# Stores of half one's sums spread over two units, x's sums and splits in another order, attention in bank 7 at a unit's first beat

## The chip, the cores and the metric

The kernel runs on one core of one Trainium2 chip. The metric is the device time of one execution in microseconds (us). Lower is better. Four compute engines work side by side, each on its own stream of instructions in program order: PE (TensorE, the matmuls), DVE (VectorE), ACT (ScalarE) and POOL (GpSimd). SP (SyncE) issues all of this kernel's DMA transfers, also in program order. Engines wait for each other by semaphores.

## The reference

A layer mixes an attention branch with a feed-forward branch, gate by gate. S = 2048 rows, D = 576, 32 heads of 18, four segments of 512 rows, 4608 hidden columns. Everything is float32.

```python
g = sigmoid((x * gate_w).sum(-1, keepdims=True))
# A: causal attention inside a segment, plus a memory of the segments before
for s in range(4):
    p = softmax(q_s @ k_s.T * scale + mask)
    a_dot = p @ v_s
    a_mem = (phi(q_s) @ M) / (phi(q_s) @ z + 1e-6)
    o = sigmoid(beta) * a_mem + (1 - sigmoid(beta)) * a_dot
    M, z = M + phi(k_s).T @ v_s, z + phi(k_s).sum()
a = concat(o) @ wo
# B: feed forward
b = (silu(x @ w_gate) * (x @ w_up)) @ w_down
out = g * a + (1 - g) * b
```

## The kernel before, in words

All float32 products are made of three cheaper ones: an operand is split into a high part (a copy on ACT that rounds) and a low part (a subtraction on DVE: `tensor_sub(lo, src, hi)`). A split is therefore always one ACT and one DVE instruction. The function `split` records both as L132 and L133, whatever is split.

The program has three stages. The first one (to about 221 us) makes q, k, v, the memory, and the splits of half of x. The second, which is the long one, runs the feed-forward branch with attention threaded through it. The third multiplies attention by `wo` and mixes.

**The second stage.** It has two halves: half one works on x's segments 2 and 3, half two on segments 0 and 1. Each half has 36 units, f = 0 to 35, one for each 128 hidden columns. A unit makes gate and up products of 1024 rows by a scheme of seven products (Strassen's): `seven(t, j)` is six matmuls of 512 columns (L1015) and one for the rest of the rows (L1018), on the operand `ops[j]` of the weights (tiles `wo_`, one DMA of 256 KB each where they are fetched from scratch memory `wc`, L709) and on `XO[j]` of x (tiles `xo`). The seven operands of x are sums of four pieces of x, split into high and low. A unit consists of eight beats: after each step the function `tick()` issues what is due. The ticks of a unit are numbered k = 0 to 7. `defer(n, fn)` puts a step n beats ahead.

**Down products.** Every third unit, at q = f % 3 = 0, sixteen groups for the three units before are put in a list (`feed`). A group is nine matmuls of 320 or 256 columns (L862) into one PSUM bank; DVE then adds the bank to the sum `ya` in SBUF (L872), which frees the bank. Two or three groups are run in a beat by the list SHARE.

**Attention.** A generator gives one step per beat or so: scores into a bank (`s_bank`, L724), a maximum over the bank on DVE (L730), exponentials on ACT (L742), a mask on POOL (L750), a split into halves on DVE and POOL (L756, L757), a transposing DMA (L761), and after five banks the products with v (`v_unit`, L772, L773).

**Banks.** PSUM has eight. `seven` uses 0, 1 and 2. Down groups take from (3, 4, 7) the one that was taken longest ago. Attention takes from (5, 6), when there are no groups from all five of (5, 6, 7, 3, 4), and, while all sixteen groups are still listed, from (5, 6, 7) (`ts_tile`). PE waits where a bank's last content is not read yet.

**Between the halves.** After unit 35 of half one, sixteen groups are left. They run in ten extra beats (BREAK). In the last unit and these beats the operands of x for half two are made by `x_second`: `load` (L986) fetches the eight pieces, `total` (L991) makes a sum on POOL, `parts` splits a piece or a sum, and the tables LOADS, SUMS and PARTS of (beat, z, piece or operand) say at which beat each is issued. Beat 0 of these tables is the first beat of unit 35, beat 8 the first extra one, beat 18 the first of half two. z says which half of the 256 rows of the contraction. The pieces with z = 1 lie in tiles `wo_`, whose places the weights of half two take next. In the first beat of half two, `tick` stores all eight tiles of half one's sums (`ffd<-ya`, L1056), and then fetches the seventh operand of that unit.

Of the kernel before, what the change touches and what calls it, by code (L numbers as in the profile page):

```python
# [27 lines left out]
FT = 36  # L28
# [7 lines left out]
CH = 3  # L36
# [12 lines left out]
SHARE = (0, 0, 2, 2, 3, 3, 3, 3)  # L49
BREAK = 10  # L50
LOADS = ((-3, 0, 0), (-2, 0, 1), (3, 1, 0), (4, 1, 3), (4, 0, 3), (5, 0, 2), (5, 1, 1), (6, 1, 2))
SUMS = ((2, 0, 1), (9, 0, 4), (10, 1, 1), (11, 1, 4), (13, 1, 2), (14, 1, 6), (17, 0, 2), (18, 0, 6))
PARTS = ((1, 0, 0), (4, 0, 1), (10, 1, 0), (12, 1, 5), (12, 1, 3), (13, 1, 1), (14, 1, 2), (15, 1, 4), (16, 1, 6),
         (16, 0, 5), (17, 0, 3), (18, 0, 2), (19, 0, 4), (20, 0, 6))
FIRST = (9, 10, 11, 15, 16, 17, 18)
SLOT = (0, 3, 2, 1, 4, 6, 5)
RPOS = (0, 1, 4, 2, 5, 6, 3)
# [9 lines left out]
def gated_mix(ctx, tc, xT, xrest, wf, wfr, wfh, wd, wv, wo, beta, cmask, ident, bmask, out):  # L67
    nc = tc.nc
# [43 lines left out]
    y_tile = banks(2)  # L112
    taken = {}
    clock = [0]

    def soonest(ids, held):
        n = min(ids, key=lambda i: taken.get(i, 0))
        clock[0] += 1
        taken[n] = clock[0] + held
        return n  # L120

    def ts_tile(shape=(P, L)):
        ids = (5, 6, 7, 3, 4) if not groups else (5, 6, 7) if groups[0][0] < FT // CH - 1 and len(groups) == 16 else (5, 6)
        return ps.tile(list(shape), F32, name=f"bank{soonest(ids, HELD)}")

    def group_tile(shape=(P, L)):
# [2 lines left out]
    groups = []  # L129
# [85 lines left out]
    def w_load(f, u):  # L215
        r = raw_tile().rearrange("p (k n) -> p k n", n=P)
        nc.sync.dma_start(r, wf[f][:, u, 0:4])
        return r
# [30 lines left out]
    def r_fetch(f):  # L249
        nc.sync.dma_start(f32(rhs[f % 2][:96]).rearrange("p j n -> p (j n)"), rc[f // 4, :, f % 4])  # L250
# [437 lines left out]
    with ExitStack() as st:  # L688
# [238 lines left out]
        def c_tr(o, me):  # L927
            if me is not None:
                nc.gpsimd.tensor_add(o[:, 0:D], o[:, 0:D], me)
            nc.gpsimd.tensor_copy(o[:, 576:640], o[:, 512:576])  # L930
            ta = half_tile([P, 4, P])
            for k in range(4):
                nc.tensor.transpose(ta[:, k], o[:, P * k:P * k + P], idt)
            tb = lone_tile([P, P])
            nc.tensor.transpose(tb, o[:, 512:640], idt)
            oh = cps[0].tile([P, 4, P], F32R, name="oh")
            ol = cps[0].tile([P, 4, P], F32R, name="ol")
            os_ = cps[0].tile([P, P], F32R, name="os")
            split(oh, ol, ta)
            xs_split(os_, tb)  # L940
            r = []
            for k in range(4):
                r += [oh[:, k], ol[:, k], oh[:, k]]
            return r + [os_, os_]


        stores = []
# [28 lines left out]
        def feed(half, f):  # L976
            return [(f // CH, i, hf, hs, ds, yas[half], half) for i in range(8) for hf in range(2)]

        def x_second(new, rest):
# [3 lines left out]
            def load(z, q):  # L983
                b, kt = ((0, z), (1, z), (0, 2 + z), (1, 2 + z))[q]
                r[z, q] = wop.tile([P, L], F32, name="wo_") if z else raw_tile()[:, :L]
                nc.sync.dma_start(r[z, q], xT[HALF[1][b], :, kt])  # L986

            def total(z, j):
                c, d, e, g = (r.get((z, q)) for q in range(4))
                o, p, q = {1: (c, d, c), 4: (d, g, d), 2: (g, g, c), 6: (e, e, g)}[j]  # L990
                nc.gpsimd.tensor_sub(o, p, q)  # L991

            def parts(z, j):
                new[j][z] = x_slot(SLOT[j], z)
                split(new[j][z][:, 0], new[j][z][:, 1], r[z, (0, 0, 3, 2, 1, 3, 2)[j]])

            def fetch(j):
                rest[j] = xr_tile(j)
                nc.sync.dma_start(f32(rest[j]), xrd[j])

            todo += [(o, lambda z=z, q=q: load(z, q)) for o, z, q in LOADS]
            todo += [(o, lambda z=z, j=j: parts(z, j)) for o, z, j in PARTS]
            todo += [(o, lambda z=z, j=j: total(z, j)) for o, z, j in SUMS]
            todo += [(6 + j, lambda j=j: fetch(j)) for j in range(7)]
# [19 lines left out]
        for pos, (half, f) in enumerate(seq):  # L1024
            if f == 0:
                yas[half] = yp.tile([P, 8, D], F32, name="ya")
            q = f % CH
            nxt = seq[pos + 1] if pos + 1 < len(seq) else None
            if q == 0 and f:
                groups += feed(half, f - 1)  # L1030
            plan = []
            if not nxt:
                plan.append((3, lambda: early.append(c_tr(*tiles.pop(0)))))
            if nxt:
                plan += w_fetch(nxt[1]) if nxt[0] and nxt[1] < KEPT else w_make(*nxt)
                if nxt != (0, 1):
                    plan.append((1 if nxt[1] else 10, lambda f=nxt[1]: r_fetch(f)))
                for n, h in enumerate(BLOCKS.get(pos, ())):
                    plan += r_block(h, 4 * n)
                if f + 2 < FT:  # L1040
                    wraw_of[f + 2] = [None, None]
                    for u in range(2):
                        plan.append(((2, 5)[u] if f or not half else 5 + u, lambda u=u, f=f: wraw_of[f + 2].__setitem__(u, w_load(f + 2, u))))
            if pos == FT - 2:
                X2, XR2 = [[None, None] for _ in range(7)], [None] * 7
                plan += [(o + 8, fn) for o, fn in x_second(X2, XR2)]
            for o, fn in plan:
                defer(o + 1, fn)
            step = [0]

            def tick():
                k = step[0]
                step[0] += 1
                if k == 0:
                    while stores:
                        nc.sync.dma_start(*stores.pop(0))  # L1056
                if half == 0:
                    if (q, k) in ((0, 3), (1, 3), (2, 2)):
                        draw[f] = d_load(f)
                    if (q, k) in ((1, 1), (1, 7), (2, 4)):  # L1060
                        g = f - 1 if k == 1 else f
                        ds[half, g] = d_split(g, draw.pop(g))
                elif (q, k) in ((1, 0), (1, 2), (2, 1)):
                    g = f - 1 if k == 0 else f
                    ds[half, g] = d_fetch(g)
                beat(k, half)

            ops, rem = wops.pop((half, f)), rhs[f % 2]
            hh = fp.tile([P, 2, L], F32R, name="hh")
            hl = fp.tile([P, 2, L], F32R, name="hl")  # L1070
            hs[half, f] = hh, hl
            a, y, xx = a_tile(), y_tile(), x_tile()
            p5, sg0, sg1 = (row_tile() for _ in range(3))
            seven(a, 0)
            nc.scalar.activation(xx, a, AF.Copy)  # L1075
            tick()
            seven(y, 1)
            nc.scalar.activation(p5, y, AF.Copy)
            tick()
            seven(a, 2, False)  # L1080
            y = y_tile()
            nc.vector.tensor_add(y, a, p5)
            tick()
            seven(xx, 3, False)
            nc.scalar.activation(sg0, xx, AF.Copy)  # L1085
            tick()
            seven(a, 4, False)
            xx = x_tile()
            nc.scalar.activation(xx, a, AF.Copy)  # L1089
            nc.vector.tensor_add(p5, a, p5)  # L1090
            tick()
            nc.scalar.activation(sg0, sg0, AF.Silu)  # L1092
            seven(y, 5, False)
            nc.scalar.activation(sg1, y, AF.Silu)
            if f < FT - 1:
                exp_table()
            tick()
            tick()
            seven(xx, 6, False)
            nc.vector.tensor_mul(sg0, xx, sg0)  # L1100
            nc.vector.tensor_mul(sg1, p5, sg1)
            if q == CH - 1:
                defer(2, lambda t=(hh[:, 0], hl[:, 0], sg0): split(*t))
            else:
                split_by(2, hh[:, 0], hl[:, 0], sg0)
            split_by(3, hh[:, 1], hl[:, 1], sg1)
            tick()
            assert not groups
            if f == FT - 1:
                groups += feed(half, f)  # L1110
                if half == 0:
                    for n in range(BREAK):
                        beat(None if n > 1 else n)
                        if n == 0:
                            down_parts([groups.pop(0) for _ in range(3)], CH - 1, CH)
                    XO, XR = X2, XR2
                    assert not groups
# [98 lines left out]
```

## Time and profile before

| | |
|---|---|
| median of 3 runs | 1736.47 us (1733.69 to 1738.83) |
| the profiled execution: its own time | 1734.02 us |
| its span from first to last instruction | 1732.2 us |
| granted TensorE clock, mean | 0.999 |
| busy: PE, DVE, ACT, POOL | 1713.1, 1373.7, 1092.4, 936.7 us |
| half one's last unit, the extra beats, half two's first unit | 912 to 925, 925 to 947.7, 947.7 to 965.9 us |

A row of the timeline gives start, duration, engine, line, operation, written and read tiles, and in brackets the idle time of the engine before it with what ended it. A matmul's end is modelled: the next one on PE starts 0.23 us after a matmul of 512 columns, though that one's row says 0.39. Rows that follow each other on one line and tile are merged (x6).

### The profile page before, as it was taken

To read this page: it belongs to the slowest core of one execution; us is meant where nothing else is said; L and a number is where in the kernel's file an instruction comes from. 1 tells how busy PE (TensorE), PEld (TensorE's weight loads), DVE (VectorE), ACT (ScalarE), POOL (GpSimd) and SP (SyncE) were. 2 spreads that over 40 slices of the span, in tenths; PEclk is the share of its full clock that TensorE was granted. 3 is DMA by queue.
4 is the path that set the end of the run, shared out by engine and by line. 5 is a ranking of instruction groups with operands and counts; after the bars stand their busy time and mean duration, and the time that the engine had idled before them with its cause. 6 is when DMAs were issued, how large, how long until landed. Compare 5 with 4: busy or idle time off the path is not lost.

```text
span 1732.2 us, 34907 instructions
## 1 busy us (share of the span) xinstructions
PE 1713.1 (99%) x11868; PEld 1479.3 (85%) x11868; DVE 1373.7 (79%) x3231; ACT 1092.4 (63%) x2195; POOL 936.7 (54%) x1194
## 2 busy tenths in 40 slices
PE   9999999999999999999999999999999999999999
PEld 7899978888888888887888788888888888888899
DVE  6667588888898889898989677788788777888655
ACT  7766585776677577667756756665765576566511
POOL 4424645666666556565666455555555555555221
PEclk9999999999999999999999999999999999999999
DMA  8654499999898898897979976876778677766544
GB/s 285 227 194 154 146 311 191 223 218 193 208 227 194 178 213 198 190 194 200 206 150 260 273 161 146 183 180 157 157 181 181 137 161 182 163 144 166 160 146 137
DMA packets 524002, 328.05 MB, mean 189 GB/s; under 512 B 411184, under 2 KB 460336, under 8 KB 523824
## 3 DMA queue, kind: packets, MB, share of 16 engines
q1 hardware_dynamic: 523824, 325.83, 76.6%
q8 instruction: 93, 1.52, 0.4%
q14 instruction: 85, 0.70, 0.1%
HBM read 165.76 MB, written 76.09 MB: 140 GB/s over the span
## 4 chain that ended last, share of the span: by engine, by line
PE 80%; ACT 6%; DVE 6%; DMA 3%; issue 2%; POOL 1%; SPq 1%; DVEq 0%; ACTq 0%; POOLq 0%
PE bank L1015 31%; PE bank L862 25%; PE bank L155 10%; PE bank L1018 5%; PE bank L724 4%; PE bank L772 2%; PE bank L773 1%; ACT L1092 1%; PE bank L410 1%; DVE scr L730 1%; DVE hl L957 1%; DVE p L756 1%; PE bank L456 1%; ACT L1008 1%; DVE xo L133 1%
## 5 line engine op out<-in xcount | busy, mean ns | idle before, releaser
L757 POOL TENSOR_TENSOR p<-pe,p 128x512 f16<-128x512 f32 x320 | 374.0, 1169 | 451.0 <-DVE p L756 431.3
L862 PE MATMUL bank<-dw,hh 128*128 128x320 f32 (+1 forms) x2304 | 489.7, 305 | 2.6 <-DVE ya L872 2.1
L862 PEld LDWEIGHTS bank<-dw,hh 128*128 128x128 f32 x2304 | 380.5, 190 | 16.7 <-DVE ya L872 5.7
L742 ACT ACTIVATE pe<-bank,mb 128x512 f32<-128x512 f32 (+3 forms) x512 | 246.0, 522 | 218.7 <-DVE mb L730 213.3
L862 PE MATMUL bank<-dw,hl 128*128 128x320 f32 (+1 forms) x1152 | 340.3, 295 | 0.2 <-DVE hl L133 0.2
L730 DVE CUSTOM_DVE_ANT_0 scr<-bank,cm 128x512 bf16<-128x512 f32 (+3 forms) x512 | 246.5, 481 | 7.8 <-PE bank L724 1.1
L862 PEld LDWEIGHTS bank<-dw,hl 128*128 128x128 f32 x1152 | 217.9, 189 | 0.4 <-DVE hl L133 0.4
L872 DVE TENSOR_TENSOR ya<-bank,ya 128x320 f32<-128x320 f32 x352 | 157.6, 453 | 71.5 <-PE bank L862 70.6
L1018 PE MATMUL bank<-xr,rh 128*128 128x512 f32 x504 | 196.5, 390 | 0.0
L750 POOL TENSOR_SCALAR_AFFINE_SELECT pe<-pe 128x256 f32<-128x256 f32 (+1 forms) x320 | 151.1, 473 | 30.4 <-ACT pe L742 20.1
L756 DVE CAST p<-pe 128x512 f16<-128x512 f32 x320 | 149.2, 466 | 0.0
L260 POOL TENSOR_TENSOR ws<-raw 128x256 f32<-128x256 f32 x140 | 123.5, 882 | 17.3 <-DMA raw<-in_wf_dram 5.1
L724 PE MATMUL bank<-kst,qst 108*128 108x512 bf16 (+3 forms) x512 | 125.5, 306 | 0.0
L1018 PEld LDWEIGHTS bank<-xr,rh 128*128 128x128 f32 x504 | 94.7, 188 | 20.5
L957 DVE TENSOR_TENSOR hl<-row,hh 128x512 fp32r<-128x512 f32 x120 | 101.9, 849 | 10.8 <-ACT hh L956 10.5
L1085 ACT ACTIVATE row<-bank 128x512 f32<-128x512 f32 x72 | 43.1, 598 | 83.9 <-PE bank L1018 83.8
L1092 ACT ACT_TABLE_LOAD x72 | 92.4, 1283 | 1.3
L1090 DVE TENSOR_TENSOR row<-bank,row 128x512 f32<-128x512 f32 x72 | 49.6, 689 | 54.6 <-ACT bank L1089 54.4
L1008 ACT ACT_TABLE_LOAD x70 | 89.8, 1283 | 1.0
L1089 ACT ACTIVATE bank<-bank 128x512 f32<-128x512 f32 x72 | 42.0, 584 | 67.2 <-PE bank L1018 66.8
L155 PE MATMUL bank<-xo,qhi 128*128 128x512 f32 x264 | 83.1, 396 | 0.3 <-ACT vps L395 0.3
L1075 ACT ACTIVATE bank<-bank 128x512 f32<-128x512 f32 x72 | 41.6, 578 | 66.2 <-PE bank L1018 66.2
(2167 smaller groups left out, 4137.6 us busy)
## 6 DMA issues: line engine op xcount, KB each, us to landing
raw<-in_wf_dram SPq DMA_DIRECT2D x140, 256.0 KB
rh<-rc SPq DMA_DIRECT2D x72, 336.0 KB
dc<-dw SPq DMA_DIRECT2D x36, 576.0 KB
dw<-dc SPq DMA_DIRECT2D x36, 576.0 KB
stk<-q SPq DMA_DIRECT2D x32, 384.0 KB
draw<-in_wd_dram SPq DMA_DIRECT2D x36, 288.0 KB
rc<-rt SPq DMA_DIRECT2D x42, 224.0 KB
vd<-vps SPq DMA_DIRECT2D x8, 912.0 KB
```

Of the source, the lines that this page charges most:

```text
L155: nc.tensor.matmul(t, st[n], mv[n], start=(n == 0), stop=(n == 13))
L260: (nc.gpsimd.tensor_sub if sub else nc.gpsimd.tensor_add)(src[j], p(), q())
L724: nc.tensor.matmul(t[:, c:c + w], qs[:KR, pr, P * i:P * i + P], ks[:KR, pr, 0:w], start=True, stop=True)
L730: nc.vector.tensor_tensor_reduce(scr[:, :w], t[:, c:c + w], cm[:, L - w:L], -SCALE, 3.0e38, OP.add, OP.min, m[:, k:k + 1])
L742: nc.scalar.activation(pe[:, c:c + w], t[:, c:c + w], AF.Exp, bias=m[:, k:k + 1], scale=SCALE)
L750: nc.gpsimd.affine_select(d, d, pattern=pat, compare_op=OP.is_ge, fill=0.0, base=0, channel_multiplier=1)
L756: nc.vector.tensor_copy(p[:, 0], pe)
L757: nc.gpsimd.tensor_sub(p[:, 1], pe, p[:, 0])
L862: nc.tensor.matmul(ts[m], p, q[:, cs], start=(n == 0), stop=(n == 3 * CH - 1))
L872: nc.vector.tensor_add(ya[:, i, cs], t, ya[:, i, cs])
L1015: nc.tensor.matmul(t, w[:, p, z], x[z][:, q], start=first and n == 0, stop=False, skip_group_check=True)
L1018: nc.tensor.matmul(t, rem[:, RPOS[j]], XR[j], start=False, stop=True, skip_group_check=True)
```

## The change

Three edits go together. First, `tick` no longer issues all eight stores ahead of the first beat of half two, but at most one at each odd beat: four in the unit (1,0), four in (1,1). Second, SUMS and PARTS give the sums and splits of `x_second` another order: the splits of z = 0 that need no sum come in the first extra beats, and the others follow in the order in which half two needs them. Third, `ts_tile` chooses differently: with groups in the list attention has banks 5 and 6 only, but the first attention bank after a feed is bank 7 (unless bank 7 was the last bank taken, or the feed is that of a half's last units). The down groups' own choice among 3, 4 and 7 follows from that.

```diff
-PARTS = ((1, 0, 0), (4, 0, 1), (10, 1, 0), (12, 1, 5), ...
+PARTS = ((1, 0, 0), (4, 0, 1), (8, 0, 5), (9, 0, 3), (10, 1, 0), ...
+    fed = []
     def ts_tile(shape=(P, L)):
-        ids = (5, 6, 7, 3, 4) if not groups else (5, 6, 7) if groups[0][0] < FT // CH - 1 and len(groups) == 16 else (5, 6)
+        ids = (5, 6) if groups else (5, 6, 7, 3, 4)
+        if fed and groups[0][0] < FT // CH - 1 and max(taken, key=taken.get) != 7:
+            ids = (7,)
+        fed.clear()
         return ps.tile(list(shape), F32, name=f"bank{soonest(ids, HELD)}")
@@
             if q == 0 and f:
                 groups += feed(half, f - 1)
+                fed.append(f)
@@ def tick():
-                if k == 0:
-                    while stores:
-                        nc.sync.dma_start(*stores.pop(0))
+                if k % 2 and stores:
+                    nc.sync.dma_start(*stores.pop(0))
```

The engines' orders differ in three places and in the banks; in all else they are the same. The lines of the new program stand four (or five) higher, so that L1015 is L1019 there.

On SP, at the start of half two (`wo` is an operand of the weights, `ffd` a store, `pt` a transposing DMA of attention, `rh` the weights' rest rows), before:

```order
L709 DMA wo__13368<-wc 128x512
L808 DMA kst_2324<-stk 18x2x512 x2
L1056 DMA ffd<-ya 128x576 x8
L709 DMA wo__13415<-wc 128x512
L250 DMA rh_2332<-rc 96x896
L761 DMA_TRANSPOSE pt<-p 128x8x128
L709 DMA wo__13457<-wc 128x512
L709 DMA wo__13467<-wc 128x512
```

And after, from the same place:

```order
L713 DMA wo__13372<-wc 128x512
L812 DMA kst_2324<-stk 18x2x512 x2
L713 DMA wo__13410<-wc 128x512
L1060 DMA ffd<-ya 128x576
L254 DMA rh_2332<-rc 96x896
L765 DMA_TRANSPOSE pt<-p 128x8x128
L713 DMA wo__13450<-wc 128x512
L1060 DMA ffd<-ya 128x576
L713 DMA wo__13461<-wc 128x512
L765 DMA_TRANSPOSE pt<-p 128x8x128
```

The fetch of the seventh operand (13415 before, 13410 after) moved ahead of all stores, and each later fetch has one to four stores ahead of it instead of eight.

On ACT, around the first extra beat (`hh` is the high part of unit 35's hidden tile, which the down groups need; `xo<-raw` and `xo<-wo` are splits of x; `row` the hidden tile), before:

```order
L1094 ACTIVATE row<-bank_12920 128x512
L132 ACTIVATE hh<-row 128x512
L742 ACT_TABLE_LOAD
L742 ACTIVATE pe<-bank_12987,mb_2326 128x128
L742 ACTIVATE pe<-bank_12987,mb_2326 128x384
L956 ACTIVATE hh<-row 128x512
```

And after:

```order
L1098 ACTIVATE row<-bank_12920 128x512
L136 ACTIVATE xo_13023<-raw 128x512
L136 ACTIVATE hh<-row 128x512
L746 ACT_TABLE_LOAD
L746 ACTIVATE pe<-bank_12987,mb_2326 128x128
L746 ACTIVATE pe<-bank_12987,mb_2326 128x384
L136 ACTIVATE xo_13080<-raw 128x512
L960 ACTIVATE hh<-row 128x512
```

Two splits of x (operands 5 and 3, z = 0) moved ahead, the first in front of the split of the hidden tile; on DVE their low parts moved along, and the first stands in front of `hl` there too.

On PE, in a unit of half one that begins with sixteen groups (f = 21; here buffer numbers are kept, and the digit after `bank` is the bank), rows picked before:

```order
L724 MATMUL bank7_8609<-kst1_2324,qst1_2323 128x512
...
L862 MATMUL bank3_8636<-dw_8240,hh_7662 128x320 x2
...
L862 MATMUL bank4_8662<-dw_8240,hh_7662 128x256 x2
...
L862 MATMUL bank3_8691<-dw_8240,hh_7662 128x320 x2
...
L862 MATMUL bank7_8722<-dw_8240,hh_7662 128x256 x2
```

And after:

```order
L728 MATMUL bank6_8609<-kst1_2324,qst1_2323 128x512
...
L866 MATMUL bank3_8636<-dw_8240,hh_7662 128x320 x2
...
L866 MATMUL bank4_8662<-dw_8240,hh_7662 128x256 x2
...
L866 MATMUL bank7_8691<-dw_8240,hh_7662 128x320 x2
...
L866 MATMUL bank3_8722<-dw_8240,hh_7662 128x256 x2
```

The order of the matmuls is the same, but the third group of the unit now goes to bank 7, which attention filled at the unit's first beat, instead of back to bank 3, which the first group had filled.

More of the change, by code (lines that the diff above doesn't have):

```diff
@@ L51 @@
 LOADS = ((-3, 0, 0), (-2, 0, 1), (3, 1, 0), (4, 1, 3), (4, 0, 3), (5, 0, 2), (5, 1, 1), (6, 1, 2))
-SUMS = ((2, 0, 1), (9, 0, 4), (10, 1, 1), (11, 1, 4), (13, 1, 2), (14, 1, 6), (17, 0, 2), (18, 0, 6))
-PARTS = ((1, 0, 0), (4, 0, 1), (10, 1, 0), (12, 1, 5), (12, 1, 3), (13, 1, 1), (14, 1, 2), (15, 1, 4), (16, 1, 6),
-         (16, 0, 5), (17, 0, 3), (18, 0, 2), (19, 0, 4), (20, 0, 6))
+SUMS = ((2, 0, 1), (9, 0, 4), (11, 0, 2), (12, 1, 1), (13, 1, 4), (14, 0, 6), (14, 1, 2), (16, 1, 6))
+PARTS = ((1, 0, 0), (4, 0, 1), (8, 0, 5), (9, 0, 3), (10, 1, 0), (11, 1, 5), (12, 1, 3), (13, 0, 4), (14, 0, 2),
+         (15, 1, 1), (16, 1, 4), (17, 1, 2), (18, 0, 6), (19, 1, 6))
 FIRST = (9, 10, 11, 15, 16, 17, 18)
```

## The prediction

> **What bounds the kernel now.** I read the page first, then PE's waits, then the stretch in which most of them lie.
>
> ```profile
> span 1732.2 us, 34907 instructions
> PE 1713.1 (99%) x11868; PEld 1479.3 (85%) x11868; DVE 1373.7 (79%) x3231; ACT 1092.4 (63%) x2195; POOL 936.7 (54%) x1194
> ```
>
> PE is busy for all but 19.1 us of the span. The change takes no matmul away and adds none, so a gain can only come from PE's waits, or from matmuls that run at a lower clock. The list of PE's waits names them:
>
> ```profile
> PE bank L1015 <- DMA wo__13415<-wc: 3.0, 1, 3.0
> PE bank L862 <- DVE ya L872: 2.1, 3, 0.9
> PE bank L1015 <- ACT bank L1075: 1.7, 5, 0.6
> PE bank L1015 <- DVE bank L1082: 1.6, 2, 1.1
> PE bank L1015 <- DVE xo L133: 0.9, 1, 0.9
> ```
>
> The first, second and fifth lie where the change works. Third and fourth are waits inside a unit on ACT and DVE, which it doesn't touch.
>
> **The stores.** PE's timeline at the start of half two, then SP's, then the busy time by stretch:
>
> ```profile
> 951.17 0.48 PE L1015 MATMUL bank<-xo,wo__13172 128*128 128x512 f32 x1
> 952.57 1.42 PE L1015 MATMUL bank<-xo,wo__13172 128*128 128x512 f32 x5 [0.92 <-DVE xo L133]
> ...
> 959.77 0.39 PE L1018 MATMUL bank<-xr,rh 128*128 128x512 f32 x1
> 963.11 2.60 PE L1015 MATMUL bank<-xo,wo__13415 128*128 128x512 f32 x6 [2.95 <-DMA wo__13415<-wc]
> ...
> 965.93 1.98 PE L1015 MATMUL bank<-xo,wo__13457 128*128 128x512 f32 x6
> 967.75 0.40 PE L1018 MATMUL bank<-xr,rh 128*128 128x512 f32 x1
> 967.99 0.39 PE L724 MATMUL bank<-kst,qst 108*128 108x512 bf16 x1
> ```
> ```profile
> 952.24 5.49 SPq L1056 DMA_DIRECT2D ffd<-ya  x8
> 957.82 0.88 SPq L709 DMA_DIRECT2D wo__13415<-wc  x1
> 958.76 1.06 SPq L250 DMA_DIRECT2D rh<-rc  x1
> 959.92 1.24 SPq L761 DMA_TRANSPOSE pt<-p  x1
> 961.26 0.61 SPq L709 DMA_DIRECT2D wo__13457<-wc  x1
> ```
> ```profile
> 960.00:963.00 3.00, 0.16 (x1) 0.00 (x0) 0.00 (x0) 2.96 (x5) 0.00 (x0) 1.00 1.00 232
> 963.00:967.00 4.00, 3.89 (x10) 3.10 (x11) 0.76 (x2) 0.19 (x1) 0.00 (x0) 0.57 1.10 279
> ```
>
> A matmul follows a full one after 0.23 us (967.75 to 967.99). So PE could have gone on at 959.77 + 0.23 = 960.00 and went on at 963.11: 3.1 us lost. In the second stretch the granted clock (the third figure from the end) is 0.57, after 1.00 before it: of 4 us at 0.57, 4 x 0.43 = 1.7 us are lost too. The stall costs 4.8 us. SP's rows show its cause: eight stores keep SP from 952.24 to 957.73, and the fetch stands behind them. It takes from 957.82 to 963.1, 5.3 us, and is the last thing PE waits for.
>
> After the change this fetch is issued where the first store stood, at about 952.3, and lands at about 957.6 by the same 5.3 us. PE wants it at 960.0, or 1.2 us earlier if the wait at 952.57 goes. That leaves 1.2 us at least. What is late next: the following unit's first tile, 13457. Before it on SP stand one store, the rest rows and a transposing DMA, which takes 1.24 us once its data are there. 952.3 + 0.9 (the fetch) + 0.7 (a store, 5.49 / 8) + 1.1 + 1.2 = 956.2, with 5.3 more 961.5. PE wants it at 965.93 - 4.8 - 1.2 + 2.4 (the loss below) = 962.3. That is close, and the transposing DMA may wait for POOL. The gain of this edit is between 2 and 4.8 us; I take 4.8, since each sum comes out ahead of PE.
>
> The Trainium skill (TensorE: Matmul & The Clock Gate, "What's actually happening") says that PE falls to half its clock after an idle window of about 3.4 us, and that the window runs freely. The trace has the drop after 2.95 us of idle, a little less than a window. By that rule alone no clock would have been lost here and this term would be 3.1 us.
>
> **x's sums and splits.** The wait at 952.57 is for the low part of operand 2: 952.57 - 951.17 - 0.23 = 1.2 us. In the new order both splits of operand 2 are out in the extra beats, and what is left for half two's first unit is operand 6, which PE needs three steps later. So 1.2 us go.
>
> But the first extra beat now has a split of a raw piece in front of the hidden tile's, on ACT and on DVE alike. When does that piece land? SP, ACT, DVE, PE:
>
> ```profile
> 924.53 0.43 SPq L986 DMA_DIRECT2D raw<-in_xT_dram  x1
> ...
> 928.58 0.32 SPq L999 DMA_DIRECT2D xr<-xrd  x1
> ```
> ```profile
> SPq L999 <- DMA raw<-in_xT_dram: 0.5, 1, 0.5
> ```
> ```profile
> 926.34 0.58 ACT L1094 ACTIVATE row<-bank 128x512 f32<-128x512 f32 x1
> 927.20 0.63 ACT L132 ACTIVATE hh<-row 128x512 fp32r<-128x512 f32 x1 [0.28 <-DVE row L1100]
> 927.85 1.28 ACT L742 ACT_TABLE_LOAD   x1
> 929.14 0.84 ACT L742 ACTIVATE pe<-bank,mb 128x128 f32<-128x128 f32 x2
> ```
> ```profile
> 927.86 0.69 DVE L133 TENSOR_TENSOR hl<-row,hh 128x512 fp32r<-128x512 f32 x1
> ...
> 928.61 0.42 PE L862 MATMUL bank<-dw,hl 128*128 128x320 f32 x1 [0.16 <-DVE hl L133]
> ```
>
> The raw piece of operand 5 is issued at 924.53, and an issue on SP at 928.58 had waited for it: it lands 4.0 us after its issue. Nothing before it on SP moves, so it lands then in the new program too. ACT is free at 926.92, and its work is in order: it must wait until 928.58 to split that piece, then for 0.5 us, and only then comes `hh`, at 929.1 instead of 927.20. On DVE the low part of the piece goes ahead of `hl`: it starts when ACT has ended, at 929.2, and `hl` 0.6 us later, at 929.8 instead of 927.86. PE waited for `hl` at 928.61 already, with nothing to do. So 2.0 us are added to that wait. Behind the waiting `hh` on ACT stand a table load and the exponentials, for which attention waits; they are late by the same 1.9 us, and since PE is late too, no second wait follows.
>
> DVE then has another moved split (operand 3) ahead of the sums that free the down groups' banks. In the extra beats DVE is as full as PE, and its instructions beside a POOL one take longer:
>
> ```profile
> 936.00:947.00 11.00, 11.00 (x85) 10.89 (x84) 10.66 (x24) 4.93 (x10) 8.34 (x7) 1.00 1.13 267
> ```
> ```profile
> 930.75 1.29 DVE L756 CAST p<-pe 128x512 f16<-128x512 f32 x1
> ...
> 941.31 0.41 DVE L756 CAST p<-pe 128x512 f16<-128x512 f32 x1
> ```
>
> A split takes 0.69 us there (the `hl` row). The same conversion is 0.41 us alone and 1.29 beside POOL's sum, so the split may grow by 0.9. Splits that come early are not there later: the count in the extra beats stays eight behind `hl`. I take 0.4 us, with 0 and 1.6 as the ends. Together this edit costs 2.0 + 0.4 - 1.2 = 1.2 us. At the lower end the piece is there in time, and it gains 1.2; at the upper end PE's idle time of 2.0 us lowers the clock as 3 us did at 963 (1.7 more) and DVE is late by 1.6: a loss of 4.1.
>
> The Trainium skill (SBUF — State Buffer, "SBUF: two separate sides") says that a DVE instruction with two SBUF inputs and a POOL one that reads SBUF shut each other out for the whole instruction. The 1.29 us beside 0.41 look like that. By this rule a moved split pays up to a whole sum on POOL more, which would put the 0.4 near its upper end of 1.6.
>
> **Bank 7.** The third group of a unit at f = 21:
>
> ```profile
> 631.46 0.39 PE L1018 MATMUL bank<-xr,rh 128*128 128x512 f32 x1
> 632.75 0.56 PE L862 MATMUL bank<-dw,hh 128*128 128x320 f32 x2 [0.91 <-DVE ya L872]
> ```
> ```profile
> L862 PE MATMUL bank<-dw,hh 128*128 128x320 f32 (+1 forms) x2304 | 489.7, 305 | 2.6 <-DVE ya L872 2.1
> L742 ACT ACTIVATE pe<-bank,mb 128x512 f32<-128x512 f32 (+3 forms) x512 | 246.0, 522 | 218.7 <-DVE mb L730 213.3
> L730 DVE CUSTOM_DVE_ANT_0 scr<-bank,cm 128x512 bf16<-128x512 f32 (+3 forms) x512 | 246.5, 481 | 7.8 <-PE bank L724 1.1
> ```
>
> This group goes to bank 3, which the first group filled and DVE has not yet read. PE loses 632.75 - 631.46 - 0.23 = 1.06 us. The same place waits in eight units; their idle time is the 2.6 us of the group's row, and since each begins 0.16 us before the modelled end (0.39 - 0.23), 8 x 0.16 = 1.3 come on top: 3.9 us. After the change the group finds bank 7, which attention filled at the unit's first beat, over 5 us earlier; its readers need 0.48 and 0.52 us. So the waits go. The next group takes bank 3 with a group in between, 1.4 us later, which is more than the longest wait. In the fourteen other such units PE runs on from there with no wait. I take 3.9; the ends are 1.5 (the lateness of DVE shows up in later groups) and 4.2.
>
> **The sum.** -4.8 + 1.2 - 3.9 = -7.5 us. The profiled execution took 1734.02 us (1732.2 of span and 1.8 around it), the median of three is 1736.47. From the execution's own time the sum gives 1726.5, from the median 1729.0; I take the middle, 1728.
>
> **The rivals.** *No loss in the extra beats*: the raw piece lands earlier, or DVE takes it up. For it: the landing is read through another wait. Then -4.8 - 1.2 - 3.9 = -9.9, 1725.6.
>
> *The wait for weights only moves on* to the next unit's tiles, behind stores and transposing DMAs. For it: the margin of 0.8 us at the first tile, and a DMA share of 1.00 and 1.10 in the rows, so the transfers have no room. Against it: the same transfers are spread wider. About 2.5 us of stall come back, or the bank waits come back as others: -7.5 + 2.5 to + 4, 1730.5 to 1732.
>
> *Slower*: bank 7 is a bad bank for attention. All of attention in those units then has banks 5 and 6 alone, and 22 units pay. If a bank is not read when PE comes for it, PE waits at the head of its queue, for 0.5 us as the down groups do now (3.9 / 8): 22 x 0.5 = 11 us, -7.5 + 11 = +3.5, 1739. With 0.9, the longest in the waits' row, it is +12.3, 1748. It decides against the change from 0.34 us a unit on (7.5 / 22). Against it: attention's group on L724 is in none of PE's waits, and a bank is read 1.0 us of work after it is filled.
>
> *The change does little*: all terms at their weak ends, -2 + 4.1 - 1.5 = +0.6, 1736.
>
> **How the numbers follow.** Forecast 0.56, no loss in the extra beats 0.12, the wait moves on 0.18, slower by bank 7 0.08, little 0.06. A measurement of this kernel tells about 0.3%, 5.2 us, from no change. Faster by that: most of the forecast (0.46), the first rival, and some of the second: 0.62. Within it: 0.29. Slower: 0.09. The range of 1723.5 to 1733.5 goes from the first rival, less 2.1 us for the spread of the runs, to the second, with 1.5 more; it leaves out the third and part of the last.
>
> **What would show it.** Right: no wait of L1019 for a `wc` tile and a clock of 1.00 in half two's first units; no wait for `xo` there; PE waiting some 2 us for `hl` or `hh` just before the extra beats; nothing left of L866 waiting for `ya` at a third group. Wrong: attention's L728 or L776 among PE's waits in many units, or PE waiting for a tile of the unit (1,1).

## The result, and the profile after

The changed kernel takes 1731.77 us (median of 13 runs, 1729.05 to 1733.25), the kernel before 1735.9 in the same comparison (13 runs, 1733.58 to 1738.83). The ratio is 0.9974, with a 95% interval of 0.9966 to 0.9983: 4.5 us less, between 3.0 and 5.9. In this document a ratio is turned into time with 1736 us.

The two profiled executions differ by less, 1732.42 against 1734.02 us of own time: the one of before lies at the low end of that kernel's runs, the one of after in the upper half of its own. So the size is taken from the medians, and the traces say where it comes from.

The page of after begins:

```profile
span 1730.7 us, 34907 instructions
PE 1712.1 (99%) x11868; PEld 1479.6 (85%) x11868; DVE 1371.9 (79%) x3231; ACT 1092.4 (63%) x2195; POOL 934.9 (54%) x1194
```

PE's waits in after (what it waited for, us in total, times, the longest). Most lines of the program stand four lower than before: L862 is now L866, L1015 is L1019, L724 is L728.

```profile
PE bank L1019 <- DMA wo__13450<-wc: 1.6, 1, 1.6
...
PE bank L866 <- ACT hh L136: 1.6, 1, 1.6
PE bank L728 <- ACT pe L746: 1.4, 2, 1.0
...
PE bank L776 <- ACT pe L746: 1.1, 2, 0.9
...
PE bank L1022 <- DMA rh<-rc: 0.8, 2, 0.5
PE bank L866 <- DVE ya L876: 0.7, 1, 0.7
PE bank L1019 <- DMA wo__13575<-wc: 0.5, 1, 0.5
```

Three of the waits that the prediction named are gone: the 3.0 us for the seventh weight tile, the 0.9 us for operand 2 (`xo`), and the third groups' 2.1 us for `ya` (the 0.7 us left are elsewhere, at 936 us). In their place stand the seven waits above, six of which were not in the list of before: 1.6 + 1.6 + 1.4 + 1.1 + 0.8 + 0.7 + 0.5 = 7.7 us. PE's idle time is 1730.7 - 1712.1 = 18.6 us, where it was 19.1: between these two executions the waits have moved more than they have gone, and 1.0 of the 1.5 us by which the span is shorter is busy time, as matmuls that run at full clock give.

**Start of half two.** PE, the busy time by stretch (granted clock third from the end) and SP in after:

```profile
961.47 0.39 PE L1022 MATMUL bank<-xr,rh 128*128 128x512 f32 x1
963.45 1.61 PE L1019 MATMUL bank<-xo,wo__13450 128*128 128x512 f32 x6 [1.59 <-DMA wo__13450<-wc]
...
965.13 0.39 PE L728 MATMUL bank<-kst,qst 108*128 108x512 bf16 x1
```
```profile
963.00:967.00 4.00, 3.55 (x16) 2.79 (x17) 1.82 (x5) 1.40 (x4) 1.16 (x1) 1.00 1.11 380
```
```profile
953.49 0.34 SPq L713 DMA_DIRECT2D wo__13410<-wc  x1
953.88 0.43 SPq L1060 DMA_DIRECT2D ffd<-ya  x1
954.35 0.42 SPq L254 DMA_DIRECT2D rh<-rc  x1
954.87 1.75 SPq L765 DMA_TRANSPOSE pt<-p  x1
956.75 1.17 SPq L713 DMA_DIRECT2D wo__13450<-wc  x1
```

The seventh tile (13410) is issued at 953.49 and PE never waits for it; the clock stays at 1.00. The first attention matmul behind the stall starts at 965.13, where it started at 967.99 in before: 2.9 us earlier. But the next unit's first tile, 13450, lands just ahead of 963.45, some 6.7 us after its issue at 956.75, and PE waited 1.59 us for it. The lead does not last either. Matched matmul by matmul (the start of each in after less its start in before), PE is 2.9 us ahead at 965 and 0.3 us behind at 994; the waits for `rh` and 13575 in the list above lie between.

**The extra beats.** ACT and PE in after:

```profile
925.10 0.58 ACT L1098 ACTIVATE row<-bank 128x512 f32<-128x512 f32 x1
927.25 0.63 ACT L136 ACTIVATE xo<-raw 128x512 fp32r<-128x512 f32 x1 [1.57 <-DMA raw<-in_xT_dram]
927.78 0.61 ACT L136 ACTIVATE hh<-row 128x512 fp32r<-128x512 f32 x1
```
```profile
928.45 0.56 PE L866 MATMUL bank<-dw,hh 128*128 128x320 f32 x2 [1.56 <-ACT hh L136]
```

As forecast: ACT waits for the raw piece with the split of the hidden tile queued behind it, and PE waits behind ACT.

**Bank 7.** Matched in the same way, PE stands 3.0 us earlier once the third group of the unit f = 21 has run, and only 1.2 us earlier at 829 us. What is given back are PE's waits on attention, L728 and L776. The first of them, followed back by the chain of waits in after:

```profile
632.97 4.89 DMA rc<-rt
...
637.89 0.05 DVEq L251
...
639.34 0.20 DVE scr L734
...
640.25 0.84 ACT pe L746 x2
...
645.79 0.38 PE bank L728
```

L251 is the low part of the rest (`rt`, in `r_block`), on DVE. It overwrites `rt`, so it waits until the store of the high part, `rc<-rt`, has landed: 4.89 us. DVE works in order; behind it stand the maxima of attention (L734), behind those ACT's exponentials, and at 645.79 PE. DVE's waits at this one operation in before and in after (L247 and L251):

```profile
DVE rt L247 <- DMA kst<-stk: 5.7, 4, 2.4
DVE rt L247 <- DMA rc<-rt: 4.3, 5, 1.6
```
```profile
DVE rt L251 <- DMA rc<-rt: 12.2, 8, 2.5
DVE rt L251 <- DMA kst<-stk: 4.0, 3, 1.9
```

10.0 us became 16.2. The rest of DVE's work starts earlier, the landing does not.

### The profile page after: what moved, and what is told of

Same layout as the page of the kernel before. It is cut to its first block, busy times and chain, and to the rows that moved or that the text cites. A ratio compares the mean times of both kernels' runs of the same rounds, so it can differ in the third digit from the quotient of the medians.

```text
span 1730.7 us, 34907 instructions
## 1 busy us (share of the span) xinstructions
PE 1712.1 (99%) x11868; PEld 1479.6 (85%) x11868; DVE 1371.9 (79%) x3231; ACT 1092.4 (63%) x2195; POOL 934.9 (54%) x1194
## 4 chain that ended last, share of the span: by engine, by line
PE 81%; ACT 6%; DMA 5%; DVE 3%; issue 2%; POOL 2%; SPq 1%; DVEq 0%; ACTq 0%; POOLq 0%
PE bank L1019 32%; PE bank L866 24%; PE bank L159 10%; PE bank L1022 5%; PE bank L728 4%; PE bank L776 2%; PE bank L777 1%; DMA rh<-rc 1%; ACT L1096 1%; PE bank L414 1%; DMA rc<-rt 1%; ACT L1012 1%; ACT pe L746 1%; PE bank L460 1%; POOL ws L264 0%
## 5 line engine op out<-in xcount | busy, mean ns | idle before, releaser
L866 PE MATMUL bank<-dw,hh 128*128 128x320 f32 (+1 forms) x2304 | 488.9, 305 | 2.3 <-ACT hh L136 1.6
L866 PEld LDWEIGHTS bank<-dw,hh 128*128 128x128 f32 x2304 | 381.5, 190 | 14.9 <-ACT hh L136 1.8
L866 PE MATMUL bank<-dw,hl 128*128 128x320 f32 (+1 forms) x1152 | 340.6, 296 | 0.2 <-DVE hl L137 0.2
L734 DVE CUSTOM_DVE_ANT_0 scr<-bank,cm 128x512 bf16<-128x512 f32 (+3 forms) x512 | 246.4, 481 | 10.0 <-PE bank L728 3.3
L866 PEld LDWEIGHTS bank<-dw,hl 128*128 128x128 f32 x1152 | 218.0, 189 | 0.5 <-DVE hl L137 0.5
L728 PE MATMUL bank<-kst,qst 108*128 108x512 bf16 (+3 forms) x512 | 125.5, 307 | 1.4 <-ACT pe L746 1.4
L374 POOL TENSOR_TENSOR q<-qr,q 128x512 bf16<-128x512 f32 x36 | 44.4, 1234 | 70.3 <-ACT q L373 59.2
L264 POOL TENSOR_TENSOR ws<-raw,ws 128x256 f32<-128x256 f32 x70 | 56.5, 807 | 47.1 <-DVE wo__22572 L271 10.3
```

Source lines behind the costliest of these rows:

```text
L264: (nc.gpsimd.tensor_sub if sub else nc.gpsimd.tensor_add)(src[j], p(), q())
L728: nc.tensor.matmul(t[:, c:c + w], qs[:KR, pr, P * i:P * i + P], ks[:KR, pr, 0:w], start=True, stop=True)
L734: nc.vector.tensor_tensor_reduce(scr[:, :w], t[:, c:c + w], cm[:, L - w:L], -SCALE, 3.0e38, OP.add, OP.min, m[:, k:k + 1])
L866: nc.tensor.matmul(ts[m], p, q[:, cs], start=(n == 0), stop=(n == 3 * CH - 1))
```

## The experiments

The theory to test has three parts. The edits act as the prediction said, each by itself; the stores' gain is partly lost because the transfers of half two's first two units fill the DMA queue whatever their order; and bank 7's gain is partly lost at `rt`. Rivals: the edits disturb one another, so that waits come back only where they are together; or the waits of attention come from attention having two banks (the prediction's third rival).

**One edit at a time.** The kernel before with the stores alone:

```diff
-                if k == 0:
-                    while stores:
-                        nc.sync.dma_start(*stores.pop(0))
+                if k % 2 and stores:
+                    nc.sync.dma_start(*stores.pop(0))
```

> The kernel before with the stores alone spread (one at each odd beat). Theory 1, from the two traces: the 3.1 us wait for the seventh operand and its slow clock (4.8 us) go, but 4 us come back in the next unit as waits for its operands and rest rows, since the rest rows' transfer takes 2.5 us in the queue and every operand behind it lands late: -1 us against before (-2.5 to +0.5). Theory 2, the prediction's term: -4.8 us, with no wait for weights left.

Measured: 1731.42 us, ratio 0.9977 (0.9966 to 0.9987), 4.0 us less (2.3 to 5.9). That is close to theory 2 and beyond the -2.5 at which theory 1 ended, though a wait for a weight tile is left, which theory 2 did not have. PE's waits in it:

```profile
PE bank L1015 <- DMA wo__13450<-wc: 1.0, 1, 1.0
PE bank L1015 <- DVE xo L133: 0.9, 1, 0.9
```

Behind the old stall's place (967.99 in before) PE is 4.1 us earlier than in before (the same matmuls matched), with its new wait for 13450 already paid. By 994 it is only 2.5 us earlier. The edit does what was forecast for it, and gives part of it back without the other two.

With the two tables of x's order alone (`SUMS` and `PARTS` of the change):

> The kernel before with the new SUMS and PARTS alone. Both theories: PE waits about 2 us for hh and hl ahead of the extra beats, 0.4 to 0.7 us more for a bank in them, and 1.2 us less for operand 2 in half two's first unit: +1.2 us (0 to +2.5). A rival: what is lost in the extra beats is hidden by the wait for the seventh operand that follows at 963 (its landing hangs on SP, not on PE): then about 0, and the wait for it is shorter by what was lost before.

Measured: 1738.38 us, ratio 1.0011 (1.0002 to 1.0020), 1.9 us more (0.3 to 3.5), as expected. The rival does not hold: the wait for the seventh operand was 3.6 us, not shorter. ACT and PE in it:

```profile
929.73 0.63 ACT L132 ACTIVATE xo<-raw 128x512 fp32r<-128x512 f32 x1 [2.98 <-DMA raw<-in_xT_dram]
930.26 0.61 ACT L132 ACTIVATE hh<-row 128x512 fp32r<-128x512 f32 x1
```
```profile
930.93 0.55 PE L862 MATMUL bank<-dw,hh 128*128 128x320 f32 x2 [3.00 <-ACT hh L132]
```

ACT's wait for the piece and PE's for the split behind it are equal, 2.98 and 3.00 us. The operation that the order was to spare, the wait for `xo`, is gone here too.

With the bank rule alone (`ids` and `fed` of the change):

> The kernel before with the bank choice alone. Theory 1: eight waits of third groups (3.9 us) go, but 2.5 us of the 3.0 in half one come back some 13 us later as waits of attention for a bank, because DVE stands in its queue for the landing of a DMA (rc<-rt) that does not come earlier: -1.9 us (-3.5 to -0.5). Theory 2, the prediction's term: -3.9 us, nothing comes back.

Measured: 1733.35 us, ratio 0.9985 (0.9976 to 0.9994), 2.6 us less (1.0 to 4.2). The interval holds the times of both theories, so the trace has to decide. PE's waits, then DVE's, in it:

```profile
PE bank L776 <- ACT pe L746: 1.8, 3, 0.8
...
PE bank L728 <- ACT pe L746: 1.4, 2, 1.0
```
```profile
DVE rt L251 <- DMA rc<-rt: 10.4, 7, 2.8
DVE rt L251 <- DMA kst<-stk: 6.1, 4, 2.4
```

The third groups' waits are gone, and the attention waits are there without any change at half two. So it is the bank rule that calls them up.

**Stores and bank without the order:**

> Stores and bank choice together, with the old order of x's sums and splits. Theory 1: the 2.4 us in the extra beats are not paid and the 1.2 us wait for operand 2 stays; against the full change 1 us faster (-3 us against before, -1 to -5). Theory 2, by the prediction's terms: -8.7 us against before. If it is slower than the full change, the new order helps in a way that the traces do not show.

Measured: 1728.44 us, ratio 0.9961 (0.9946 to 0.9977), 6.8 us less. The three edits alone add up to -4.0 + 1.9 - 2.6 = -4.7 us, and all three together give -4.5; the first and third add up to -6.6 and give -6.8. Within the intervals (up to 2.7 us to either side) they add, so nothing speaks for the first rival. At -6.8 the pair lies between theory 1 (-3, at most -5) and theory 2 (-8.7): less comes back than theory 1 had it.

**The rest's low part a beat later.** The kernel after with

```diff
-                (o + 4, lambda: nc.vector.tensor_sub(t, a, f32(t))), (o + 5, lambda: keep(2))]
+                (o + 5, lambda: nc.vector.tensor_sub(t, a, f32(t))), (o + 6, lambda: keep(2))]
-                    plan += r_block(h, 4 * n)
+                    plan += r_block(h, 5 * n)
```

> The changed kernel with the low part of the rest rows' sums (rt, a DVE instruction that must wait until the DMA rc<-rt has read the high part) one beat later, and its store too; nothing else. Theory 1: DVE's 16 us of waits for that DMA shrink by most, the waits of attention for banks at 645, 706 and 827 go, and about 2.5 us that had come back are gained: 1729.5. Rival: those waits come from attention having two banks instead of three; then they stay, and the time is that of the changed kernel (1731.8).

Measured: 1731.15 us, ratio 0.9972 (0.9963 to 0.9981): not to be told from the kernel after. In its trace the attention waits at 645, 706 and 827 us are gone, but PE has new ones between 230 and 495 us, in the units that make two blocks of the rest and so have both of them shifted:

```profile
PE bank L1019 <- ACT bank L1079: 2.4, 6, 0.8
...
PE bank L1019 <- DVE wo__3707 L271: 0.5, 1, 0.5
PE bank L1019 <- DVE wo__4630 L271: 0.3, 1, 0.3
```

The attention waits go as theory 1 has it, but the time is the rival's, since the shift also reached units that it harmed. So the same shift only where a unit makes one block (`len(BLOCKS[pos]) < 2`), the others as in after:

> The kernel after, with the rest's low part and its last store one beat later only in units that make one block of the rest (from f = 15 on); units with two blocks are as they were. Theory 1 (VectorE stands in its queue at the rest's low part until the store before it has landed, and this gives bank 7's gain back): VectorE's waits there in single-block units go, the waits of attention at about 646, 707 and 828 us go, nothing new comes at 230 to 500 us: 2.5 to 3.0 us under the kernel after, about 1729. Rival (the beat that the work moves to is as full, and the wait only changes its place, as in the units with two blocks): other waits of 0.3 to 0.9 us between 490 and 830 us, and no more than 0.5 us under the kernel after, about 1731.5.

Measured: 1728.10 us, ratio 0.9954 (0.9940 to 0.9968), 3.5 us under the kernel after by the ratios (the intervals overlap by a hair). L728 and L776 no longer wait for ACT in its list, and no new wait of 0.3 us or more comes between 300 and 900 us. DVE's waits at `rt`:

```profile
DVE rt L251 <- DMA rc<-rt: 4.7, 4, 2.3
DVE rt L251 <- DMA kst<-stk: 4.1, 2, 2.4
```

Attention still has banks 5 and 6 alone in this kernel, as in after. So two banks alone do not make these waits, and the prediction's third rival, by which 22 units pay for them, does not hold.

**The split of the hidden tile first.** The kernel after with operands 5 and 3 split one beat later:

```diff
-(8, 0, 5), (9, 0, 3),
+(9, 0, 5), (10, 0, 3),
```

> The changed kernel with the two early splits one beat later each, so that the hidden tile's split stands first. Theory 1: PE's 1.6 us wait for hh goes and with it most of the loss that the order alone made: -1.5 to -2.5 us against the changed kernel, 1729.5 to 1730.3. Rival: it is DVE's load in the extra beats, not the landing of the raw piece: then only the place of the wait moves, from hh to a bank that DVE has not read, and the time stays.

Measured: 1731.44 us, ratio 0.9971 (0.9960 to 0.9982), no clear difference from after. The wait for `hh` is gone; PE waits later, and then the granted clock falls:

```profile
935.28 0.56 PE L866 MATMUL bank<-dw,hh 128*128 128x320 f32 x2 [2.27 <-DVE ya L876]
```
```profile
936.00:940.00 4.00, 4.00 (x20) 4.00 (x20) 3.11 (x8) 1.35 (x3) 2.96 (x3) 0.57 1.17 288
```

The rival holds: DVE is full in the extra beats (busy for all of the 6 us from 929 to 935), so a split that is pushed back meets the sums that free the banks.

**The piece earlier.** The kernel after, with the fetch of that raw piece issued ahead of the other three:

```diff
-(3, 1, 0), (4, 1, 3), (4, 0, 3),
+(3, 0, 3), (3, 1, 0), (4, 1, 3),
```

> The kernel after, with the fetch of operand 5's raw piece issued first of the four fetches of x's second pieces (at about 920.3 instead of 922.8); the splits stand where they stood. Theory 1 (PE's wait for the hidden tile's split is only the landing of that piece): the piece lands 2 to 2.5 us sooner, at about 925, ScalarE splits it as soon as it is free (925.7), the split of the hidden tile follows at 926.3, and PE's wait for it falls from 1.6 us to 0.5 or less; no clock can be lost there any more: 1 to 2 us under the kernel after, about 1730.3. Rival (VectorE is too full in the extra beats, as the kernel with the splits a beat later showed, where the wait turned up at the bank instead): the wait goes, but the one for the down groups' bank at 936 grows from 0.7 us to 2 and the time stays within 0.5 us of the kernel after, 1731.8.

Measured: 1730.01 us, ratio 0.9969 (0.9957 to 0.9981): 0.9 us under after by the ratios, 1.8 by the medians, less than the runs can settle. Its trace says more. ACT:

```profile
926.09 0.58 ACT L1098 ACTIVATE row<-bank 128x512 f32<-128x512 f32 x1
926.56 0.62 ACT L136 ACTIVATE xo<-raw 128x512 fp32r<-128x512 f32 x1
927.09 0.62 ACT L136 ACTIVATE hh<-row 128x512 fp32r<-128x512 f32 x1
```

ACT no longer waits for the piece, PE's wait of 1.56 us for `hh` is gone, and of the waits at this place 0.4 us for `hl` and 0.9 for the bank at 936 are left, against 0.2 and 0.7 in after. The rival's wait of 2 us at that bank did not come. Matched with before, PE loses 2.5 us between 925 and 945 us in after and 1.0 here. So in the traces more than half of the order's loss is the piece's landing.

**The transfers at the start of half two.** The kernel after with the stores put into unit (1,2) and later ones:

```diff
-                if k % 2 and stores:
+                if half and f > 1 and stores:
```

> The changed kernel with the eight stores one a beat in the third unit of half two, where no weights come from scratch memory. Theory 1: part of what the spread stores still cost is their traffic among the fetches: the waits for 13555, 13575 and the rest rows (972 to 992, 2.1 us) go, the first one (1.6 us at 963) stays, since the rest rows' transfer and the transposing DMA before it stay: -2 us against the changed kernel, 1729.8. Rival: those waits are SP's, behind transposing DMAs that wait for POOL; then nothing changes.

Measured: 1729.14 us, ratio 0.9962 (0.9949 to 0.9974). Then with the stores as in after, but the rest rows of unit (1,1) (`rh<-rc`) fetched in the extra beats:

```diff
+                if nxt == (1, 0):
+                    plan.append((12, lambda: r_fetch(1)))
-                if nxt != (0, 1):
+                if nxt != (0, 1) and nxt != (1, 1):
```

> The changed kernel with the rest rows of the unit (1,1) fetched in the extra beats instead of in (1,0), ahead of its first operand. Theory 1: their transfer held the queue for 2.5 us; the operand 13450 lands 2.5 us earlier and PE's 1.6 us wait for it goes: -1.6 us against the changed kernel, 1730.2. Rival: SP is held by the transposing DMA that waits for POOL's p, and by the eighth DMA before it; then the wait shrinks by 0.5 us at most.

Measured: 1729.29 us, ratio 0.9966 (0.9953 to 0.9978). Each is about 2 us under after by the ratios (2.1 and 1.4) and 2.5 by the medians; the intervals overlap after's. In both traces PE no longer waits for that first tile (13449 in the one with the stores later, where theory 1 had the wait stay).

This does not show that the bytes of the stores or of the rest rows made 13450 late. The kernel with the two splits a beat later has the transfers of after in this place, and its PE does not wait for 13450 either. SP and PE in it:

```profile
956.16 0.72 SPq L713 DMA_DIRECT2D wo__13450<-wc  x1
962.16 1.52 PE L1019 MATMUL bank<-xo,wo__13450 128*128 128x512 f32 x6
```

There the tile was at hand 6.0 us after its issue; in after it took 6.7. The same stretch (the last two figures are the DMA share and GB/s) in that kernel, then in after, and the DMA answer for it in after:

```profile
959.00:962.00 3.00, 3.00 (x15) 2.49 (x14) 0.69 (x1) 2.73 (x4) 0.00 (x0) 1.00 1.51 327
```
```profile
959.00:962.00 3.00, 2.86 (x13) 2.05 (x11) 0.72 (x2) 2.95 (x5) 0.00 (x0) 1.00 1.10 72
```
```profile
DMA packets 675, 0.21 MB, mean 72 GB/s; under 512 B 653, under 2 KB 653, under 8 KB 675
```

In after the queue was busy for these 3 us and moved little, nearly all of it in packets under 512 B. The rows of the fetches, stores and rest rows are 2 KB and longer (256 KB over 128 rows, 336 KB over 96), so the small packets point to the transposing DMA (`pt`) issued just ahead of 13450. Why it went so slowly in this execution is not shown. (From 958 us on one 16 KB packet of the instruction queue was under way for 2.7 us, in the other kernel for 1.0; whether it held up the rest is open.) In the profiled executions of the five kernels with after's order of transfers, PE's wait for 13450 was 1.6 (after), 1.3, 0.3, 0.3 and 0 us.

**What the runs point to.** Stores and bank without the order, and the rest's low part later in single-block units:

> The kernel before with the stores and the bank rule, without the new order of x's sums and splits, and with the rest's low part one beat later in units with one block. Theory 1: the terms add: the kernel with stores and bank alone was at 1728.4, and 2.5 us come off: about 1726. Rival: attention's waits at 647 and 828 us in that kernel are not VectorE's lateness from the rest: same as that kernel, 1728 to 1729.

Measured: 1726.15 us, ratio 0.9944 (0.9929 to 0.9958). With the stores in unit (1,2) as well:

> As the one above, and with the stores put one a beat into unit (1,2) and later ones. Theory 1 (the transfers of half two's first units lie behind the stores): in the kernel with stores and bank alone PE no longer waits for a weight tile there, so moving the stores on brings less than 0.5 us: about 1726. Rival: the stores still cost transfers room in the first units, and 2 us more come off, as they did in the kernel after: about 1724.

Measured: 1724.76 us (1723.20 to 1725.26), ratio 0.9932 (0.9919 to 0.9945): 11.8 us under the kernel before. It is the fastest kernel of the study, and its interval lies wholly below that of the changed kernel. The time is nearer to the rival than to theory 1. Whether the last step (1.4 us by the medians, 2.1 by the ratios) is real the intervals cannot say, but the traces point that way: matched with before, PE loses 1.1 us between 968 and 994 us in the kernel above and none in this one. So the spread stores seem to cost about 1 us among the first units' fetches. What PE still waits for there is operand 2, which the order would have spared:

```profile
PE bank L1019 <- DVE xo L137: 0.9, 1, 0.9
```

## Why the prediction was right or wrong

The forecast was 1728.0 us, the measurement is 1731.8: inside the range, faster, and 3.8 us short of the forecast. The gain of 0.26% lies just inside the 0.3% mark, where the forecast had put it beyond. What came is the second rival, waits that move on, at its 1730.5 to 1732.

- **The stores, -4.8.** Right in the mechanism: the fetch ahead of the stores lands in time and the clock stays at 1.00. The size is right too where 13450 is in time: matched with before (one execution of each), PE gains 4.8 us between 945 and 968 us in each of the three kernels that have the stores and the bank rule without the order, and 6.0 (4.8 and the 1.2 of operand 2) in the one with the splits a beat later. In after it gains 4.1 there and loses 3.2 from there to 994; alone the edit gave -4.0. The failed step is "I take 4.8, since each sum comes out ahead of PE": 13450 (13457 in the prediction) was reckoned to land at 961.5 for a PE that wants it at 962.3. PE wanted it at 961.7 (961.47 and 0.23), and it landed at 963.4: issued at 956.75 instead of 956.2, and 6.7 us under way instead of the 5.3 of a fetch that stood right behind the eight stores. What held it is open (above). The later tiles' waits were put at nothing. The text had named the sign ("PE waiting for a tile of the unit (1,1)").
- **x's order, +1.2.** The mechanism is shown, with the waits on ACT and PE of the same length (2.98 and 3.00; 1.57 and 1.56) and by the kernel with the piece fetched earlier. Alone it cost 1.9, within its bounds of -1.2 and +4.1. In the extra beats the sum was close: PE lost 2.5 us there in after, where 2.0 + 0.4 was forecast. The moved split of operand 3 took 1.56 us on DVE beside a sum on POOL, 0.9 more than the 0.69 of a split alone, as the prediction allowed. (It fits the rule on two inputs, which the prediction names, better than the prediction's 1.29 us row does: that one is a conversion with a single input.) The term's size hangs on when the piece lands, and that differs by run: PE's wait for `hh` was 1.6 us in after, 1.9 to 2.3 in four kernels with the same order, 3.0 in the one with the order alone. The bound that a wait of 2 us lowers the clock came true in some of them (below).
- **Bank 7, -3.9.** The waits at the third groups went as forecast: PE is 3.0 us earlier by then. Alone the edit gave -2.6. The failed step is "I take 3.9", which puts at nothing what comes behind the third group: DVE waits there for a landing that keeps its time, and attention stands behind DVE. The end of 1.5 ("the lateness of DVE shows up in later groups") had the engine right and the place wrong: it showed in attention. The waits of L728 and L776 were named as a sign of the third rival; they came, two of each, but from another cause.
- **The sum.** -7.5 was forecast; the three edits alone measured -4.7, all together -4.5. The miss of 2.8 in the single edits is 0.8, 0.7 and 1.3, each with an interval of 1.6 to 1.8 to either side, so the times alone blame no single edit. Another 1.0 of the forecast's 3.8 came from reckoning half from the profiled execution's own time, which was a low one of its kernel: from the median the same sum gave 1729.0.

## What to carry to other kernels

A wait that goes only pays if the next event on the same path does not keep its own time. Before a gain is booked, look for operations further on, on any in-order engine, that wait for a DMA to land: time won ahead of them is lost there, and the one that overwrites a tile just being stored is easily overlooked. A fetch that has been moved ahead uncovers the next one. Reckon its landing with all that was issued just ahead of it, a transposing DMA included, and leave a margin: with the same transfers ahead, 13450 took 6.7 us from issue to use in after, 6.0 at most in the kernel with the splits a beat later. And before a wait that has gone is put down to an edit, look for it in a kernel that has the same transfers without the edit.

## What the hardware showed

The granted clock falls after waits well under the 2.95 us after which it fell in before. Windows from 929 to 935 us (granted clock third from the end) in the kernel with the rest rows early, in the one with the stores later and in the one with the rest's low part later:

```profile
929.00:935.00 6.00, 4.80 (x64) 4.36 (x65) 5.67 (x13) 5.97 (x12) 3.03 (x4) 1.00 1.10 317
```
```profile
929.00:935.00 6.00, 5.18 (x58) 4.75 (x59) 5.97 (x14) 5.97 (x12) 3.43 (x4) 0.72 1.07 310
```
```profile
929.00:935.00 6.00, 4.54 (x53) 4.08 (x54) 5.29 (x13) 5.96 (x12) 2.76 (x3) 0.72 1.08 319
```

PE's waits for `hh` ahead of them were 1.9, 2.1 and 1.9 us. 0.72 over 6 us is a loss of 1.7 us, nearly as long as the wait itself, and the same as after the 2.95 us of before (0.57 over 4 us). After 1.6 us (the kernel after) the clock held, after 2.3 us it fell to 0.57 (the split pushed back), and at 1.9 us it did either. The Trainium skill (TensorE: Matmul & The Clock Gate, "What's actually happening") gives an idle window of about 3.4 us that runs freely. That it runs freely agrees with the two outcomes at 1.9 us; its length does not agree with a drop after 1.9 to 2.3 us, and the measurement decides.
